# A written-out order of instructions replaced by another, with other ways of splitting numbers in its first quarter

## The chip, the cores and the metric

The kernel runs on one core of a Trainium2 chip. A core has five engines, each with its own queue of instructions that it works through in order: TensorE (PE in the profile) multiplies matrices, VectorE (DVE), ScalarE (ACT) and GpSimd (POOL) work on elements, and SyncE (SP) issues transfers. The engines wait for one another by semaphores. The metric is the time of one execution on the device in microseconds. The kernel before has a median of 1121.21 us over three runs (1118.67 to 1121.53).

## The reference

```python
def _attn_ref(q, k, v, tau):                       # (8, 8, 576, 64) each
    scale = 1.0 / np.sqrt(q.shape[-1])
    scores = scale * np.matmul(q, k.transpose(0, 1, 3, 2))
    thresh = np.max(scores, axis=-1, keepdims=True) - tau
    scores = np.where(scores >= thresh, scores, -1000000000.0)
    scores = scores - np.max(scores, axis=-1, keepdims=True)
    attn = np.exp(scores)
    attn = attn / (np.sum(attn, axis=-1, keepdims=True) + 1e-09)
    return np.matmul(attn, v).astype(np.float32)

def _moe_ref(x, w_in, w_out):                      # (4608, 512), (512, 2048), (2048, 512)
    h = x @ w_in
    pos, neg = h >= 1.0, h <= -1.0
    g = np.where(pos, h, np.where(neg, 0.0, (h + 1.0) ** 2 / 4.0))
    return (g @ w_out).astype(np.float32)
```

Attention of 8 batches with 8 heads over 576 positions, in which scores more than tau below a row's maximum are dropped, is followed by a feed-forward network (FFN) on the 4608 tokens. The weights come as 64-bit floats, the rest as 32-bit ones.

## The kernel before, in words

Most products are computed in 16-bit floats, with each operand split into a high word (the value rounded to 16 bits) and a low word (what the rounding left, again in 16 bits). Two or three products of such words replace one in 32 bits. So nearly every operand passes through a **split**: it is scaled by a power of two, its high word is written, and the low word is the difference. Most of the change is about which engine does this.

*Heads.* They are taken in pairs, four to a batch. For each pair q and k are loaded into one of seven `raw` buffers, their squares are summed on ScalarE (line 544), a small product adds the sums up (line 552), VectorE and GpSimd derive the scales, and q and k are split. `QHOW` says how, by a letter for each pair: P means scaling on GpSimd (line 572), high word on ScalarE (578), low word on GpSimd (585); D means high word on ScalarE (576) and a *fused low word* on VectorE, scaling and difference in one instruction (583). From the second batch on the words then go by DMA into `kk` and `qq`. V is split likewise (`VHOW`: P means high words on GpSimd, line 660, and a fused low word on VectorE, 667; A the high words on ScalarE, 658; N in three steps on ScalarE and GpSimd, 651, 656 and 665) and turned by a transposing DMA. V of the first batch is turned by TensorE instead (line 698).

*Tiles.* The softmax has 288 tiles of 128 rows by 576 positions, 36 to a batch. A tile's scores (line 1005) fill one of two `s` buffers in PSUM. VectorE takes the extremum (1022) and later masks and sums (1043); ScalarE does the exponential between them (1029). `TILE` gives the way of the rest by tile number, P where it says nothing. P: normalisation on GpSimd (1061), high word on ScalarE (1074), low word on GpSimd (1077). A: the normalisation goes to ScalarE (1071). D: high word on ScalarE (1083), fused low word on VectorE (1086). S: like D, with the masked values left in PSUM (1091 to 1102). T: TensorE turns the tile through a diagonal matrix that GpSimd makes (1123, 1127), and ScalarE and VectorE split the result (1130, 1133). All but T send both words through a transposing DMA (line 1105) into `eT`, which the product with V reads (1193).

*Weights.* Both matrices come in 16 tiles of 128 by 512. Line 774 loads one; three or four instructions build 32-bit floats from the bits of the 64-bit ones (`SIGN`: N puts the low bits on GpSimd, line 795, and the sign fix on ScalarE, 788; A and D put the low bits on ScalarE, 797; D needs one VectorE instruction more, 809). A product of their own (816) gives the scale (724, 727, 746). Then `CONV` says how a tile is split. G and A: scaled, rounded and subtracted in three instructions, the first two on GpSimd (860, 866) or on ScalarE (858, 864), the third on GpSimd (869). D: high word on GpSimd (875), fused low word on VectorE (878). P, Q, R, S: high word on GpSimd (875) or ScalarE (873), the difference by two products on TensorE (881, 882), and the low word copied out by ScalarE (888) or VectorE (886). M: TensorE scales (891), ScalarE and VectorE take the words (894, 897).

*FFN.* 20 groups of at most 256 tokens run in steps of four 128-column blocks: the first product (line 1265), the gate in five instructions on ScalarE and VectorE (1271 to 1288), the second product (1310), and at its end an eviction and a store. `FSCALE` says for each batch whether the factors of the gate (lines 965 to 969) are made on VectorE or on GpSimd.

*Order.* All this is recorded as some 5,440 operations. The table `ORDER` lists their numbers in the order in which they are issued; the planner walks through it, gives each operation its buffers, and emits each engine's instructions by it. So the table fixes every queue, the transfers on SP's included. In stretches where the planner expects TensorE to wait, in the first part of the program, it inserts products of ones into a free bank (line 1344), which keep the engine's clock up. Their number follows from the table.

## Time and profile before

| what | value |
| --- | --- |
| median of three runs | 1121.21 us (1118.67 to 1121.53) |
| the profiled execution: its time, its span | 1122.48 us, 1120.7 us |
| instructions | 27229 |
| busy: TensorE, VectorE, ScalarE, GpSimd | 1091.5, 898.6, 881.3, 763.4 us |
| granted clock of TensorE, mean | 0.996 |
| read from and written to main memory | 45.09 MB, 9.44 MB |

The span reaches from the first to the last instruction. A row of the profile's groups gives line, engine and operation, output and inputs with shapes, the number of instructions, their busy time in us and the mean of one in ns, and then the idle time of the engine just before them with what ended it. An engine that is off the path that sets the end may be idle at no cost.

### The profile page before, as it was taken

The numbers are of one execution on the slowest core, as the hardware profiler recorded it, in microseconds if no ns is written. First come the engines' busy times: TensorE is split into PE (matmuls) and PEld (weight loads), VectorE is DVE, ScalarE is ACT, GpSimd is POOL, SyncE is SP. The second block draws the span as 40 slices with busy tenths as digits, with TensorE's granted clock in tenths as the row PEclk, the third lists the DMA queues.
The fourth block names the chain that finished last, engine by engine and source line by source line (L and its number), as shares of the span: only waits on it lengthen the run. The fifth ranks groups of instructions, "written<-read, shape, count | busy, mean of one in ns | idle before, by whom it ended". The sixth has DMA issues, their size and how long they took to land.

```text
span 1120.7 us, 27229 instructions
## 1 busy us (share of the span) xinstructions
PE 1091.5 (97%) x9590; PEld 767.8 (69%) x9590; DVE 898.6 (80%) x2724; ACT 881.3 (79%) x1690; POOL 763.4 (68%) x879
## 2 busy tenths in 40 slices
PE   8889989999999999999999999999999999999998
PEld 7566647766777676766777677676677676767774
DVE  5999989988899788798888888888698888876322
ACT  7999989888788888878788788777788876776343
POOL 5899877566757987678767886677696986556000
PEclk9899999999999999999999999999999999999999
DMA  9997999689969999669966999559797987646000
GB/s 350 327 230 141 159 197 186 137 157 219 172 128 159 201 188 195 146 128 213 200 98 128 201 202 177 116 115 198 160 176 147 194 149 131 116 86 127 11 20 19
DMA packets 435929, 179.41 MB, mean 160 GB/s; under 512 B 400464, under 2 KB 407632, under 8 KB 435792
## 3 DMA queue, kind: packets, MB, share of 16 engines
q1 hardware_dynamic: 435792, 177.67, 77.5%
q8 instruction: 75, 1.23, 0.5%
q14 instruction: 62, 0.51, 0.1%
HBM read 45.09 MB, written 9.44 MB: 49 GB/s over the span
## 4 chain that ended last, share of the span: by engine, by line
PE 65%; DVE 10%; ACT 9%; POOL 6%; DMA 6%; issue 4%; SPq 0%; ACTq 0%; DVEq 0%; POOLq 0%
PE acc L1310 24%; PE ph L1265 24%; PE s L1005 8%; PE ph L1193 6%; DMA eT<-hl 5%; DVE s L1022 3%; DVE e L1043 2%; POOL hl L1077 2%; ACT e L1029 2%; ACT hl L1074 2%; POOL e L1061 1%; POOL nat L585 1%; PE ph L1344 1%; POOL raw L572 1%; DVE hl L1086 1%
## 5 line engine op out<-in xcount | busy, mean ns | idle before, releaser
L1077 POOL TENSOR_TENSOR hl<-e,hl 128x576 f16<-128x576 f32 x277 | 357.4, 1296 | 137.8 <-ACT hl L1074 131.5
L1265 PE MATMUL ph<-x,WI 128*128 128x256 f16 (+1 forms) x4032 | 400.9, 257 | 1.9 <-DVE gb L1288 0.8
L1265 PEld LDWEIGHTS <-WI 128*128 128x128 f16 x4032 | 347.1, 98 | 50.7 <-issue 5.3
L1022 DVE TENSOR_SCALAR_CACHE_REDUCE s<-s,pc 128x576 f32<-128x576 f32 x288 | 233.2, 818 | 42.3 <-PE s L1005 39.3
L1043 DVE SCALAR_TENSOR_TENSOR e<-s,sm,e 128x578 f32<-128x578 f32 x286 | 232.6, 815 | 41.4 <-ACT e L1029 33.3
L1029 ACT ACTIVATE e<-s,sm 128x576 f32<-128x576 f32 x288 | 211.6, 741 | 61.9 <-DVE s L1022 42.2
L1061 POOL TENSOR_SCALAR e<-e,sm 128x576 f32<-128x576 f32 x263 | 200.2, 766 | 88.0 <-DVE sm L1053 68.2
L1074 ACT ACTIVATE hl<-e 128x576 f16<-128x576 f32 x277 | 186.9, 682 | 55.0 <-POOL e L1061 30.5
L1310 PE MATMUL acc<-WO,ga 128*128 128x512 f16 x864 | 204.3, 379 | 0.0
L1005 PE MATMUL s<-kk,qq 128*128 128x288 f16 (+3 forms) x1360 | 191.9, 286 | 11.1 <-DVE e L1043 7.1
L1005 PEld LDWEIGHTS <-qq 128*128 128x128 f16 (+3 forms) x1360 | 115.5, 99 | 69.7 <-issue 22.2
L1278 DVE SCALAR_TENSOR_TENSOR ph<-ph,fcs,asq 128x512 f32<-128x512 f32 (+1 forms) x160 | 111.5, 698 | 53.7 <-ACT asq L1274 52.8
L1271 ACT ACTIVATE asq<-ph,fcs 128x512 f32<-128x512 f32 (+1 forms) x160 | 115.7, 737 | 35.6 <-PE ph L1265 34.3
L1310 PEld LDWEIGHTS <-ga 128*128 128x128 f16 x864 | 82.3, 98 | 84.4 <-issue 3.7
L1193 PE MATMUL ph<-eT,vst 128*64 128x320 f16 (+2 forms) x1928 | 123.1, 279 | 2.1 <-DVE e L1043 1.0
L1193 PEld LDWEIGHTS <-vst 128*64 128x64 f16 x1928 | 98.8, 110 | 25.0 <-issue 14.1
L1283 ACT ACTIVATE ga<-ph,fcs 128x256 f16<-128x256 f32 (+1 forms) x160 | 70.0, 448 | 29.4 <-DVE ph L1278 25.8
L1274 ACT ACTIVATE asq<-asq 128x512 f32<-128x512 f32 x144 | 90.6, 629 | 2.7
L1288 DVE SCALAR_TENSOR_TENSOR ga<-ph,fcs,ga 128x256 f16<-128x256 f32 (+1 forms) x160 | 70.6, 450 | 26.5 <-ACT WI L1283 11.7
L1310 PE MATMUL acc<-WO,gb 128*128 128x512 f16 x300 | 72.5, 379 | 0.0
L1310 PE MATMUL acc<-WO,WI 128*128 128x512 f16 x294 | 70.8, 379 | 0.0
L585 POOL TENSOR_TENSOR nat<-raw,nat 128x576 f16<-128x576 f32 x50 | 65.0, 1302 | 6.9 <-ACT nat L578 3.5
(201 smaller groups left out, 1152.9 us busy)
## 6 DMA issues: line engine op xcount, KB each, us to landing
kk<-nat SPq DMA_DIRECT2D x112, 144.0 KB, 3.0
raw<-in_v_dram SPq DMA_DIRECT2D x32, 288.0 KB, 3.8
raw<-in_q_dram SPq DMA_DIRECT2D x32, 288.0 KB, 3.8
raw<-in_k_dram SPq DMA_DIRECT2D x32, 288.0 KB, 3.4
WO<-in_moe_w_in_dram SPq DMA_DIRECT2D x16, 512.0 KB, 7.9
out_dram<-ob SPq DMA_DIRECT2D x32, 256.0 KB, 2.7
qq<-nat SPq DMA_DIRECT2D x112, 72.0 KB, 2.6
x<-in_moe_w_out_dram SPq DMA_DIRECT2D x10, 512.0 KB, 6.4
```

The costliest lines, as they stand in the source:

```text
L1005: T.matmul(ap(s, s_ps)[r, f, :SH], q, k, start=ql == kl == 0, stop=kl == 1)
L1022: V.tensor_scalar(sv(), sv(), c[:, 24 + v : 25 + v], None, ALU.mult, ALU.min, accum_out=t[:, 0:1])
L1029: A.activation(ev(), sv(), AF.Exp, bias=ap(m, sm)[:, 0:1], scale=-1.0)
L1043: V.scalar_tensor_tensor(ev(SH + 1), sv(SH + 1), t[:, 2:3], ev(SH + 1), ALU.is_le, ALU.mult, accum_out=t[:, 3:4])
L1061: G.tensor_scalar(ev(), ev(), ap(m, sm)[:, 5:6], ESC, ALU.mult, ALU.mult)
L1074: A.activation(part2(0), ev(), AF.Copy)
L1077: G.tensor_tensor(part2(w), ev(), part2(0), ALU.subtract)
L1193: T.matmul(o[hd * D : (hd + 1) * D, :n], vt[:, k, hd * D : (hd + 1) * D], t[:, kb, hd * n : (hd + 1) * n], start=m == 0, stop=m == len(blo ...
L1265: T.matmul(h[:, i], WTh["i"][:, u, wl * 512 + c * P : wl * 512 + (c + 1) * P], x[:, cc, xl, c0 : c0 + n].rearrange("p (t n) -> p t n", n=P ...
L1271: A.activation(tv()[:, :, c], hv()[:, :, c], AF.Relu, bias=fcs[:, b, 2, q : q + 1], scale=fcs[:, b, 3, q : q + 1])
L1278: V.scalar_tensor_tensor(hv()[:, :, c], hv()[:, :, c], fcs[:, b, 0, q : q + 1], tv()[:, :, c], ALU.max, ALU.min)
L1310: T.matmul(ap(ab, accs), gv(h, gl)[:, x], WTh["o"][:, fc + i, wl * 512 : (wl + 1) * 512], start=fc + i == 0 and m == 0, stop=not left[0] a ...
```

## The change

The table of the order is another one throughout, since the numbers of the operations shift as soon as one tile takes another way. Beside it the letters change. No function changes. The first run of clock-keeping products has 106 instead of 95, all together 260 instead of 199.

```diff
-CONV = {"i": "GRPGPDPPMPGRMPPP", "o": "GAPADMMARGDGGDMA"}
-SIGN = {"i": "NNADNNNAANNNAANN", "o": "ANNNAANNAANNNNNN"}
-VHOW = "PPPPAAN" + 25 * "P"
-QHOW = "DDPDPPDPPDD" + 21 * "P"
+CONV = {"i": "GAMGMGARPMGGMGRG", "o": "PGQAGPRGRDQGRADG"}
+SIGN = {"i": "DNNNANNNNDAANNAN", "o": "NNANANAAAANNNAAN"}
+VHOW = "PPPPPPPA" + 24 * "P"
+QHOW = "DDPDPPDPPPD" + 21 * "P"
...
 ORDER = [
-    0, 54, 56, 58, 60, 855, 860, 850, 865, 4, 59, 5, 57, 55, 2, 876, 61, 871, 1, 62, 63, 16, 64, 856, 857, 80, 862, 858, 861, 65, 17, 81, 863, 852,
+    54, 0, 58, 4, 60, 56, 862, 851, 5, 55, 857, 59, 867, 2, 877, 61, 872, 57, 1, 62, 887, 63, 64, 863, 882, 864, 80, 6, 852, 865, 853, 17, 75, 854,
...
-TILE = {0: "T", 1: "T", 4: "A", 10: "A", 11: "A", 12: "A", 20: "A", 21: "A", 22: "A", 24: "A", 25: "D", 27: "A", 28: "A", 29: "A", 30: "D", 34: "D", 37: "A", 38: "A", 39: "D", 43: "A", 49: "D", 52: "D", 55: "D", 59: "D", 60: "D"}
-FSCALE = "GGVVVVVV"
+TILE = {0: "T", 1: "T", 2: "A", 4: "D", 5: "A", 9: "A", 14: "A", 15: "A", 19: "A", 20: "A", 21: "A", 22: "A", 24: "D", 25: "A", 26: "A", 27: "A", 28: "A", 29: "A", 31: "D", 33: "A", 34: "A", 36: "A", 38: "A", 39: "A", 45: "A", 50: "A", 56: "A", 58: "D", 59: "A", 60: "D", 71: "S"}
+FSCALE = "GVVVVVVV"
```

Counted over the program, weight tiles split in three steps on GpSimd go from 7 to 12 (line 860), high words alone there from 13 to 7 (875), low words by TensorE from 12 to 10 (881), products that scale from 5 to 4 (891), fused low words of weights from 4 to 2 (878), of q and k from 12 to 10 (583), of tiles from 9 to 5 (1086). Tiles normalised on ScalarE go from 14 to 23 (1071), on GpSimd from 263 to 257 (1061). Shifts of single columns (lines 736 and 961) stand in both kernels in the same number.

The first place is GpSimd's queue from the first weight tiles to the diagonal of the first tile, `dge`; `WI` holds the first weights, `dgw` a diagonal of their scale. Before:

```order
L746 TENSOR_SCALAR dgw_133<-ident,wsc_i 128x128
L860 TENSOR_SCALAR WI<-WI,wsc_i 128x512
L866 TENSOR_SCALAR WI<-WI 128x512
L869 TENSOR_TENSOR WI<-WI 128x512
L860 TENSOR_SCALAR WI<-WI,wsc_i 128x512
L795 TENSOR_SCALAR WO<-WO 128x512
L520 TENSOR_SCALAR pc_117<-pc_117 128x3
L521 TENSOR_TENSOR pc_117<-pc_117 128x3
L564 TENSOR_TENSOR pc_117<-pc_117,tcs 128x2
L1123 TENSOR_SCALAR dge_135<-ident,sm_122 128x128
```

And now:

```order
L795 TENSOR_SCALAR WO<-WO 128x512 x2
L860 TENSOR_SCALAR WI<-WI,wsc_i 128x512
L746 TENSOR_SCALAR dgw_133<-ident,wsc_i 128x128
L866 TENSOR_SCALAR WI<-WI 128x512
L860 TENSOR_SCALAR WI<-WI,wsc_i 128x512
L795 TENSOR_SCALAR WO<-WO 128x512
L869 TENSOR_TENSOR WI<-WI 128x512 x2
L866 TENSOR_SCALAR WI<-WI 128x512
L564 TENSOR_TENSOR pc_117<-pc_117,tcs 128x2
L869 TENSOR_TENSOR WI<-WI 128x512
L1123 TENSOR_SCALAR dge_135<-ident,sm_122 128x128
```

Two more subtractions (line 869) and one more rounding (line 866) stand ahead of the diagonal, and the small scale columns (lines 520 and 521) come behind it.

The second place is VectorE's queue from the first turned tile (line 1133, which frees a score buffer `s`) to the extremum of the third tile (line 1022). Before:

```order
L1133 TENSOR_TENSOR eT_98<-s_62,eT_98 128x5x128
L803 SCALAR_TENSOR_TENSOR WI<-ph_64,WO 128x512
L1133 TENSOR_TENSOR eT_98<-s_61,eT_98 128x5x128
L457 TENSOR_SCALAR ph_63<-ph_63 128x6
L458 TENSOR_SCALAR ph_63<-ph_63 128x6
L459 TENSOR_SCALAR pc_119<-ph_63 128x6
L559 TENSOR_SCALAR pc_119<-ph_63 128x6
L878 SCALAR_TENSOR_TENSOR WI<-WI,wsc_i 128x512
L803 SCALAR_TENSOR_TENSOR WI<-ph_64,WO 128x512
L803 SCALAR_TENSOR_TENSOR WI<-ph_65,WO 128x512
L1022 TENSOR_SCALAR s_61,sm_124<-s_61,pc_117 128x2x288
```

And now:

```order
L1133 TENSOR_TENSOR eT_98<-s_61,eT_98 128x5x128
L809 SCALAR_TENSOR_TENSOR WI<-WO,ph_65 128x512
L805 SCALAR_TENSOR_TENSOR WI<-WO,ph_63 128x512
L805 SCALAR_TENSOR_TENSOR WI<-WO,ph_64 128x512
L961 TENSOR_SCALAR scs<-scs 128x1 x2
L1133 TENSOR_TENSOR eT_98<-s_62,eT_98 128x5x128
L803 SCALAR_TENSOR_TENSOR WI<-ph_63,WO 128x512
L583 SCALAR_TENSOR_TENSOR qq_84<-raw_70,pc_118,qq_84 128x576
L803 SCALAR_TENSOR_TENSOR WI<-ph_65,WO 128x512
L1022 TENSOR_SCALAR s_61,sm_124<-s_61,pc_117 128x2x288
```

Three instructions on the bits of weights and two columns now stand between the two turned tiles, where one stood, and a low word of q (line 583) follows in place of one of weights (line 878).

The third place is VectorE's queue where the two orders meet; `ga` and `gb` are buffers of the gate's output. Before:

```order
L1288 SCALAR_TENSOR_TENSOR ga_110<-ph_63,fcs,ga_110 128x256
L1288 SCALAR_TENSOR_TENSOR gb_113<-ph_63,fcs,gb_113 128x256
L1278 SCALAR_TENSOR_TENSOR ph_64<-ph_64,fcs,asq_100 128x512
L583 SCALAR_TENSOR_TENSOR nat_76<-raw_75,pc_118,nat_76 128x576
L1026 TENSOR_SCALAR sm_124<-sm_124,tcs 128x1
L1288 SCALAR_TENSOR_TENSOR ga_108<-ph_64,fcs,ga_108 128x256
L1288 SCALAR_TENSOR_TENSOR gb_114<-ph_64,fcs,gb_114 128x256
L1043 SCALAR_TENSOR_TENSOR e_94,sm_124<-s_61,sm_124,e_94 128x578
```

And now:

```order
L1288 SCALAR_TENSOR_TENSOR WO<-ph_65,fcs,WO 128x256
L1278 SCALAR_TENSOR_TENSOR ph_64<-ph_64,fcs,asq_101 128x512
L1053 RECIPROCAL sm_126<-sm_126 128x1
L1022 TENSOR_SCALAR s_61,sm_122<-s_61,pc_121 128x2x288
L1026 TENSOR_SCALAR sm_122<-sm_122,tcs 128x1
L1288 SCALAR_TENSOR_TENSOR ga_109<-ph_64,fcs,ga_109 128x256
L1288 SCALAR_TENSOR_TENSOR gb_113<-ph_64,fcs,gb_113 128x256
L1043 SCALAR_TENSOR_TENSOR e_94,sm_122<-s_61,sm_122,e_94 128x578
```

From line 1026 on, the fifth row before and now, the rows are the same in both to the end, but for the numbers of the buffers. The other engines have such a place too; on SP it lies 438 rows from the end.

## The prediction

> **What bounds the kernel now.** I read the page first, for its busy shares and for the chain that ended last.

> ```profile
> PE 1091.5 (97%) x9590; PEld 767.8 (69%) x9590; DVE 898.6 (80%) x2724; ACT 881.3 (79%) x1690; POOL 763.4 (68%) x879
> ...
> PE 65%; DVE 10%; ACT 9%; POOL 6%; DMA 6%; issue 4%; SPq 0%; ACTq 0%; DVEq 0%; POOLq 0%
> ```

> TensorE is busy for 1091.5 of 1120.7 us, and two thirds of the chain is its own work. What can still be won is therefore TensorE's idle time and work taken off it. Where the idle time lies is shown by the busy time of each engine in stretches (columns: stretch, its length, then each engine's busy us with its instructions, granted clock, DMA share, GB/s).

> ```profile
> 0.00:28.00 28.00, 22.92 (x255) 19.68 (x256) 15.85 (x49) 20.51 (x44) 15.28 (x55) 0.99 0.94 350
> 28.00:56.00 28.00, 23.43 (x167) 14.20 (x167) 25.75 (x89) 26.06 (x51) 24.09 (x35) 0.89 0.90 327
> 56.00:84.00 28.00, 24.91 (x319) 17.29 (x317) 27.16 (x97) 26.52 (x51) 26.50 (x36) 1.00 1.01 230
> 84.00:112.00 28.00, 25.53 (x355) 19.22 (x353) 26.35 (x91) 27.62 (x56) 26.37 (x30) 1.00 0.80 142
> 112.00:140.00 28.00, 26.71 (x309) 19.16 (x307) 26.70 (x77) 25.58 (x46) 23.10 (x28) 1.00 0.92 159
> 140.00:168.00 28.00, 25.00 (x172) 13.48 (x171) 23.89 (x79) 24.97 (x49) 19.89 (x23) 1.00 0.95 197
> 168.00:196.00 28.00, 27.15 (x232) 21.03 (x230) 26.50 (x77) 25.21 (x46) 20.17 (x23) 1.00 1.01 186
> 196.00:224.00 28.00, 27.80 (x264) 20.82 (x263) 26.92 (x83) 23.44 (x45) 14.85 (x15) 1.00 0.68 137
> 448.00:560.00 112.00, 112.00 (x916) 78.22 (x915) 94.13 (x286) 90.19 (x170) 85.93 (x94) 1.00 0.87 171
> 1092.00:1121.00 29.00, 23.93 (x171) 13.04 (x168) 8.35 (x24) 10.79 (x27) 0.00 (x0) 0.97 0.07 19
> ```

> Up to 196 us TensorE is idle for 5.1 + 4.6 + 3.1 + 2.5 + 1.3 + 3.0 + 0.9 = 20.4 us. From 196 us on it is all but full (27.80 of 28, later 112.00 of 112), until the last 29 us, where 5.1 us go to the last gates and the last store. So there are two regimes. In the first 196 us the other engines set the pace: from 28 to 112 us VectorE is busy for 79.3 of 84 us, ScalarE for 80.2 and GpSimd for 77.0. Afterwards TensorE does. The waits say the same of the first regime (columns: who waited for whom, us in total, times, longest).

> ```profile
> PE s L1005 <- DVE e L1043: 7.1, 13, 1.2
> ...
> PE s L1127 <- POOL dge L1123: 1.3, 1, 1.3
> ```

> The score matmuls wait for VectorE to free one of the two score buffers; that is the largest wait of TensorE, and it is small and scattered. How far the softmax tiles have come is counted by their first VectorE instruction, which the profile shows as two records to a tile:

> ```profile
> 0.00:112.00 112.00, 21.44 (x50) 0.97 0.91 262
> 112.00:196.00 84.00, 21.45 (x50) 1.00 0.96 181
> 196.00:224.00 28.00, 8.72 (x20) 1.00 0.68 137
> ```

> So some 25 tiles have passed at 112 us, 50 at 196 us and 60 at 224 us. I use this to turn places in the order into times.

> **The change part by part.** The first finding comes from the order alone: on every engine the rows after a certain place are the same in both kernels but for the turn of the buffers. On VectorE these are the last 1480 or so rows, on ScalarE the last 1120, on GpSimd the last 608; on TensorE everything from the score matmuls that stand at about 277 us of the profile. The place on VectorE lies at tile 75 (the low word of line 583 just ahead of it), and that on TensorE behind an attention product:

> ```profile
> 272.08 0.81 DVE L583 SCALAR_TENSOR_TENSOR nat<-raw,pc,nat 128x576 f16<-128x576 f32 x1
> ...
> 275.56 2.09 PE L1193 MATMUL ph<-eT,vst 128*64 128x320 f16 x28
> ```

> There TensorE is already full. So the 840 us behind it, the end included, cost what they cost now, and the change is worth exactly what TensorE gains or loses before 277 us. I take the terms in that part.

> *TensorE's own work.* Two weight tiles fewer have their low word made by TensorE (line 881 and 882), and one fewer is scaled there (line 891); the clock-keeping matmuls of line 1344 grow from 199 to 260.

> ```profile
> L1344 PE MATMUL ph<-ones 128*128 128x128 bf16 x179 | 13.5, 243 | 2.4 <-POOL ones L468 2.3
> L881 PE MATMUL ph<-WI,dgw 128*128 128x512 f32 x20 | 12.1, 687 | 1.6 <-ACT WI L888 1.3 <-DVE WO L805 0.3
> L882 PE MATMUL ph<-WI,minus 128*128 128x512 f16 x10 | 4.0, 404 | 0.0
> L891 PE MATMUL ph<-WI,dgw 128*128 128x512 f32 x4 | 2.2, 632 | 0.1
> ```

> An fp32 matmul is two records, so one pass of line 881 costs 12.1 / 10 = 1.21 us, one of line 882 0.40, one of line 891 2.2 / 2 = 1.1. Removed: 2 x (1.21 + 0.40) + 1.1 = 4.3 us. Added: 61 x 13.5 / 179 = 4.6 us of clock-keeping, all of it before 84 us, where TensorE has 12.7 us of idle time to put it in. Up to the scores of tile 56 these are the only lines of TensorE whose counts differ; from there to the common part the two queues hold the same matmuls. What are 4.3 us less work worth? At most -4.3 us, if TensorE set the pace before tile 56, and 0 if it waits for others all the way. The nearest row is the wait for VectorE (7.1 us), and the splits fall where TensorE idles 20.4 us. I take 0 and keep -4.3 for the range.

> *The start.* The first run of clock-keeping matmuls grows from 95 to 106, and the matmul that sums V's squares (line 633) stands behind it in the queue.

> ```profile
> 2.32 7.57 PE L1344 MATMUL ph<-ones 128*128 128x128 bf16 x95 [2.32 <-POOL ones L468]
> 8.63 0.18 ACT L627 ACTIVATION_READ_ACCUMULATOR junk<-raw 128x1 f32 x1
> 9.73 0.17 PE L633 MATMUL ph<-vssq,ones 128*128 128x4 bf16 x1
> ```

> The last square was read out at 8.81 us, and line 633 began only at 9.73, when the 95 were through: the filling already sets this start. Eleven more at 7.57 / 95 = 0.08 us make it 0.9 us later, and VectorE and GpSimd both begin on its result. Term: +0.9 us. It would be 0 if the queues behind it had slack to give back.

> *VectorE before tile 56.* I counted its rows up to the first instruction of tile 56 in both orders, each at its mean.

> ```profile
> L667 DVE SCALAR_TENSOR_TENSOR vb<-raw,scs,vb 128x576 f16<-128x576 f32 x27 | 31.6, 1171 | 0.9 <-POOL vb L660 0.5 <-issue 0.3
> L1086 DVE SCALAR_TENSOR_TENSOR hl<-e,sm,hl 128x576 f16<-128x576 f32 x9 | 8.8, 986 | 0.5 <-POOL pc L520 0.4
> L878 DVE SCALAR_TENSOR_TENSOR WO<-WO,wsc_o 128x512 f16<-128x512 f32 x3 | 3.3, 1106 | 0.0
> L897 DVE TENSOR_TENSOR WO<-ph,WO 128x512 f16<-128x512 f32 x3 | 2.1, 684 | 0.0
> ```

> The after order has there two fused low words of tiles fewer (-2.0) and two of weights fewer (-2.1), but one of V more (+1.2), two low words from TensorE's output more and one less (+0.7; line 886 is not in this trace, and I give it line 897's 0.68), one more gate of the FFN (+0.7), one more softmax mask (+0.9), one more scale of line 965 to 969 on VectorE (+0.9 by then) and one weight tile more whose sign takes two steps (+0.7); the rest are one-column instructions (+1.9 together). The net is +2.9 us at tile 56; it is +3.7 at tile 20, +2.6 at tile 44, and -2.1 where the orders meet, since its lighter tiles come late. A mean also counts overlap with the next instruction: two records of a tile's minimum have 818 + 141 ns by their means and 21.44 / 25 = 858 ns by the stretch above, 0.89 of it. So VectorE, which is 94% busy and on which the score buffers wait, reaches tile 56 about 2.9 x 0.89 = 2.6 us later. Bounds: 0, if its idle time of 6.9 us between 112 and 196 us (84 - 26.70 - 23.89 - 26.50) takes it all, and +3.3 for tile 20. I let 1.0 us be taken up there: +1.6 us.

> *ScalarE* has 3.2 us more by tile 56, mostly six or seven more normalisations (line 1071):

> ```profile
> L1071 ACT ACTIVATE e<-e,sm 128x576 f32<-128x576 f32 x14 | 11.0, 786 | 0.0
> ```

> That lies beside VectorE's extra and is of its size; I add nothing for it. Without that cover it would be the 3.2 us itself.

> *GpSimd.* Five more weight tiles are split here in three steps and six fewer in one.

> ```profile
> L869 POOL TENSOR_TENSOR WI<-WI 128x512 f16<-128x512 f32 x3 | 3.5, 1159 | 0.2
> L860 POOL TENSOR_SCALAR WI<-WI,wsc_i 128x512 f32<-128x512 f32 x3 | 2.1, 694 | 0.0
> L866 POOL TENSOR_SCALAR WO<-WO 128x512 f16<-128x512 f32 x4 | 2.8, 712 | 0.3
> L875 POOL TENSOR_SCALAR WI<-WI,wsc_i 128x512 f16<-128x512 f32 x9 | 6.2, 695 | 0.3
> L1061 POOL TENSOR_SCALAR e<-e,sm 128x576 f32<-128x576 f32 x263 | 200.2, 766 | 88.0 <-DVE sm L1053 68.2 <-DVE sm L1026 7.8 <-ACT asq L1271 3.4
> ```

> Up to tile 36 that is 5 x (1.16 + 0.70 + 0.71) - 6 x 0.70 = +8.7 us, with three duplications of V more (+3.7), five normalisations fewer (-3.8) and three conversions of raw bits fewer (-2.0): about +7 us, and by the full count +7.8. By tile 16, near 80 us, it is +4.5. GpSimd is idle for 5.4 us from 28 to 84 us and for 20.1 us from 28 to 168 us, so the extra just fits, and I cost it at 0. It hides under VectorE's own 94%; if its idle time cannot be used, it costs what the second rival says. One place is exposed: the diagonal of the first tile (line 1123) now stands behind two more subtractions of line 869, 2.3 us, and TensorE waited 1.3 us for it already. VectorE's rows before the first two tiles are freed grow as well, by 4 us, so both arrive late together.

> *The clock.* In two slices the clock was down while TensorE was in demand:

> ```profile
> 28.00:32.00 4.00, 4.00 (x24) 2.98 (x23) 2.96 (x9) 3.16 (x7) 3.50 (x5) 0.67 0.99 364
> 36.00:40.00 4.00, 3.69 (x18) 1.94 (x18) 3.90 (x12) 3.96 (x8) 3.55 (x8) 0.68 1.04 412
> ```

> TensorE lost 4 x (0.33 + 0.32) = 2.6 us there, and VectorE stood idle for 1.04 us in the first slice. The after order has fewer splits on TensorE and more filling at this place. I take back VectorE's 1.0 us; the bounds are 0 and -2.6.

> *Contention.* A fused low word of line 1086 took 0.80 to 1.81 us:

> ```profile
> L1086 DVE SCALAR_TENSOR_TENSOR hl<-e,sm,hl x9: 801/818/1806, 111.7 to 231.8; 128x576 f16<-128x576 f32 x9
> ```

> The mean of 0.986 stands 0.17 above the median; eight fewer of lines 1086, 878 and 583 save some 1.4 us of stretching, which their means above include. [...]

> The single-column shifts of the change's name are in both kernels alike (the same counts on lines 736 and 961) and cost nothing. Weight scales on GpSimd (line 965) go from two to one.

> **The sum**: 0 + 0.9 + 1.6 + 0 - 1.0 = +1.5 us. The profiled execution took 1122.48 us (span 1120.7), 1.3 us above the median of the three runs, 1121.21. Against its own time the changed kernel would take 1124.0; against the median 1122.7. A measurement of this kernel can tell about 0.3%, 3.4 us, from no change, so the forecast is no change.

> **The rivals.** *TensorE sets the pace from 84 us on.* For it: 25.53, 26.71, 25.00 and 27.15 of 28 us, and the waits for VectorE are short. Then the 4.3 us of removed work come off, the late VectorE rows hide, and with the clock's 2.6 and the start's 0.9 it is -4.3 to -6.0: 1115 to 1117 us, faster. Against it: VectorE and ScalarE are as full in these stretches, and the removed splits lie mostly before 84 us, where TensorE idles.

> *GpSimd becomes the bound from 40 to 140 us.* Its subtractions (line 1077) feed the transposes, and its splits feed the first FFN steps. It decides once GpSimd's idle time of 5.4 us between 28 and 84 us cannot fall below 0.9 us: +4.5 us by then, +7.8 at tile 36. Part of the 7.8 is given back between 140 and 224 us, where it idles for 8.1, 7.8 and 13.2 us. With the start's 0.9 the time is 1126 to 1130 us, slower. For it: 26.50 and 26.37 of 28 us already, in order and full of waits for ScalarE. Against it: the normalisations moved off it, and its place in the waits of TensorE is one wait of 1.3 us.

> *The new order has a bad place of its own*, a late load or a transpose queued behind another in the common ring of buffers. In order of time the chain of now holds this transpose among others:

> ```profile
> 152.26 5.00 DMA eT<-hl
> ```

> One such exposed is +5 us, one removed is -5.

> *The change does nothing because nothing of it lies on the path* gives 1121 and cannot be told from the forecast.

> **How the numbers follow.** Forecast, with the case of nothing: 0.43. TensorE sets the pace: 0.22. GpSimd becomes the bound: 0.22. A bad or a mended place: 0.13, in halves a little to the slow side. That gives 0.27 for faster by over 0.3%, 0.43 for within, 0.30 for slower. The forecast's own range is 1119 to 1125; since the other cases hold over half, the range reaches from TensorE's 1115.5 to 1130, the upper end of GpSimd's.

> **What would show it.** Right: the same idle of TensorE behind 280 us; line 633 at 10.6 us; tile 56 later by 1 to 3 us; TensorE's idle up to 196 us near 20.4 plus the 4.3 us of work removed. TensorE's pace: that idle stays at 20 us, and the common part begins earlier than 277 us. GpSimd's: over 27.5 of 28 us busy from 56 to 112 us, and waits of ScalarE or TensorE for lines 1061, 1077 or 1123 that grow by microseconds. Wrong altogether: differences that arise behind 300 us, where the orders agree.

## The result and the profile after

The changed kernel took 1130.30 us (median of four runs, 1128.08 to 1132.49), the kernel before, run beside it, 1121.37 us (1118.67 to 1121.84). The ratio is 1.0071, with an interval of 1.0045 to 1.0096. The change made the kernel slower by about 0.7%, 8 to 9 us. The forecast was 1122.7 and no change; the result lies 0.3 us above the upper end of its range.

The profiled execution took 1129.07 us, with a span of 1127.3 us, 6.6 more than before. The page's first row:

```profile
PE 1097.0 (97%) x9643; PEld 774.1 (69%) x9643; DVE 895.9 (79%) x2731; ACT 884.3 (78%) x1695; POOL 772.7 (69%) x883
```

TensorE is busy for longer than before (1091.5 us), although 4.3 us of its work, by the rows before, were taken off. The products of ones took 20.9 us where they took 14.9, so 6.0 us more and not the 4.6 that their number gave. This is the largest of their rows:

```profile
L1344 PE MATMUL ph<-ones 128*128 128x128 bf16 x239 | 19.4, 248 | 3.0 <-POOL ones L468 2.3 <-DVE WI L803 0.7
```

The stretches (columns as in the prediction) show where:

```profile
0.00:28.00 28.00, 23.53 (x241) 19.13 (x242) 15.57 (x48) 20.03 (x44) 16.13 (x55) 0.90 0.96 352
28.00:56.00 28.00, 21.44 (x224) 14.92 (x223) 25.83 (x95) 26.66 (x50) 25.51 (x39) 0.97 0.82 295
56.00:84.00 28.00, 24.66 (x206) 15.03 (x206) 24.50 (x81) 24.16 (x45) 22.18 (x30) 0.64 0.93 232
84.00:112.00 28.00, 27.47 (x416) 22.78 (x415) 24.71 (x91) 25.35 (x51) 25.57 (x30) 0.94 0.79 139
112.00:140.00 28.00, 26.89 (x264) 17.30 (x262) 26.72 (x85) 26.89 (x49) 24.82 (x27) 1.00 0.82 151
140.00:168.00 28.00, 25.09 (x225) 16.11 (x223) 23.97 (x75) 24.28 (x48) 20.13 (x24) 1.00 1.03 182
168.00:196.00 28.00, 27.34 (x230) 20.24 (x229) 24.80 (x74) 24.81 (x44) 19.84 (x20) 1.00 1.10 196
```

TensorE's idle time up to 196 us is 19.6 us, where it was 20.4, so it does not wait for longer. But its granted clock is 0.90 from 0 to 28 us, where it was 0.99, and 0.64 from 56 to 84 us, where it was 1.00. In the latter stretch VectorE, ScalarE and GpSimd are busy for 24.50, 24.16 and 22.18 of 28 us, where they were for 27.16, 26.52 and 26.50. In a finer cut, two stretches of the changed kernel and then the same of the kernel before:

```profile
57.00:75.00 18.00, 16.73 (x103) 9.33 (x100) 14.66 (x48) 14.53 (x26) 13.23 (x16) 0.53 0.95 235
81.00:88.00 7.00, 7.00 (x63) 5.97 (x61) 6.64 (x21) 5.38 (x10) 6.50 (x13) 0.53 0.94 244
```

```profile
57.00:75.00 18.00, 14.91 (x176) 9.33 (x173) 17.56 (x64) 17.76 (x34) 17.32 (x22) 1.00 0.96 232
81.00:88.00 7.00, 5.79 (x97) 4.71 (x95) 6.01 (x20) 6.07 (x12) 6.41 (x12) 1.00 1.05 182
```

In these two spells TensorE ran at half clock, for 17 us and for 7 us. It was busy almost without a break there, and the others waited for it. A spell that is as long as the second lies earlier, from 22.7 to 29.5 us, and makes the 0.90 of the first stretch:

```profile
23.00:29.00 6.00, 6.00 (x35) 3.95 (x35) 5.54 (x18) 5.35 (x13) 5.74 (x8) 0.50 1.04 405
```

In the kernel before, the only spells until the very end were two of 3.4 us, from 27.2 and from 37.5 us on. The waits from 57 to 75 us in the changed kernel (who waited for whom, us, times, longest):

```profile
DVE s L1022 <- PE s L1005: 2.4, 2, 1.7
...
ACT WI L888 <- PE ph L882: 1.6, 1, 1.6
...
ACT ph L797 <- PE ph L1344: 0.9, 1, 0.9
```

VectorE waited for scores, ScalarE for a low word made on TensorE, and ScalarE also for a bank in which products of ones (line 1344) were still running. In the kernel before, no wait for TensorE is listed there. Just ahead of the two later spells, and in them, TensorE's rows in order of time (start, us, the instructions, and in brackets the idle time before them) are these:

```profile
54.65 0.91 PE L1005 MATMUL s<-kk,qq 64*128 64x288 f16 x6 [0.72 <-DVE e L1043]
55.92 0.89 PE L1005 MATMUL s<-kk,qq 64*128 64x288 f16 x6 [0.36 <-DVE e L1043]
...
60.20 1.60 PE L1005 MATMUL s<-kk,qq 64*128 64x288 f16 x6 [1.27 <-DVE e L1043]
...
78.82 1.03 PE L1193 MATMUL ph<-eT,vst 128*64 128x128 f16 x30 [2.06 <-DVE WO L805]
...
83.27 4.87 PE L1265 MATMUL ph<-x,WI 128*128 128x128 f16 x48
```

Single microseconds of the same trace date the spells (columns as above):

```profile
56.00:57.00 1.00, 1.00 (x9) 0.65 (x9) 1.00 (x2) 0.92 (x3) 0.74 (x2) 0.91 0.88 344
57.00:58.00 1.00, 1.00 (x13) 1.00 (x11) 1.00 (x4) 0.71 (x1) 1.00 (x1) 0.50 1.01 414
73.00:74.00 1.00, 1.00 (x6) 0.40 (x4) 0.00 (x0) 1.00 (x3) 0.25 (x1) 0.56 1.04 283
74.00:75.00 1.00, 1.00 (x11) 0.70 (x10) 0.90 (x5) 1.00 (x3) 0.00 (x0) 1.00 1.07 196
80.00:81.00 1.00, 1.00 (x10) 0.68 (x9) 1.00 (x2) 1.00 (x5) 1.00 (x2) 0.85 0.65 70
```

TensorE waited 0.72 and 0.36 us, and the clock fell at about 56.8 us; it came back near 73.9. TensorE waited 2.06 us, and the clock fell at 80.7. The first FFN step (line 1265) took 4.87 us, where it took 2.84 before.

The product behind which the two queues are alike began 5.1 us later than before (275.56 us), and the rest of the span is 1.5 us longer. TensorE's row of it:

```profile
280.65 2.09 PE L1193 MATMUL ph<-eT,vst 128*64 128x320 f16 x28
```

In this pair of executions the start got hardly later. Line 633 began at 9.80 us, where it began at 9.73, since the 106 products of ones took 7.64 us, where the 95 took 7.57 (rows in order of time):

```profile
2.33 7.64 PE L1344 MATMUL ph<-ones 128*128 128x128 bf16 x106 [2.33 <-POOL ones L468]
9.80 0.17 PE L633 MATMUL ph<-vssq,ones 128*128 128x4 bf16 x1
```

So the question for the experiments was whether the half clock was the cause or only went along with another one: GpSimd's extra splits, or the order itself.

### The profile page after: what moved, and what is told of

Its sections match the earlier page's. It is cut to its first block, busy times and chain, and to the rows that moved or that the text cites. A ratio compares the mean times of both kernels' runs of the same rounds, so it can differ in the third digit from the quotient of the medians.

```text
span 1127.3 us, 27377 instructions
## 1 busy us (share of the span) xinstructions
PE 1097.0 (97%) x9643; PEld 774.1 (69%) x9643; DVE 895.9 (79%) x2731; ACT 884.3 (78%) x1695; POOL 772.7 (69%) x883
## 4 chain that ended last, share of the span: by engine, by line
PE 71%; DVE 7%; DMA 7%; POOL 6%; ACT 5%; issue 3%; SPq 0%; ACTq 0%; POOLq 0%; DVEq 0%
PE ph L1265 26%; PE acc L1310 26%; PE s L1005 10%; PE ph L1193 7%; DMA eT<-hl 4%; POOL hl L1077 2%; DVE s L1022 2%; DVE e L1043 2%; POOL e L1061 1%; DMA raw<-in_q_dram 1%; ACT hl L1074 1%; PE ph L1344 1%; DMA WO<-in_moe_w_in_dram 1%; ACT e L1029 1%; ACT asq L1271 1%
## 5 line engine op out<-in xcount | busy, mean ns | idle before, releaser
L1043 DVE SCALAR_TENSOR_TENSOR e<-s,sm,e 128x578 f32<-128x578 f32 x285 | 231.8, 815 | 37.9 <-ACT e L1029 29.3
L1061 POOL TENSOR_SCALAR e<-e,sm 128x576 f32<-128x576 f32 x257 | 195.8, 767 | 91.8 <-DVE sm L1053 73.0
L1005 PE MATMUL s<-kk,qq 128*128 128x288 f16 (+3 forms) x1360 | 193.0, 290 | 11.3 <-DVE e L1043 9.6
L1005 PEld LDWEIGHTS <-qq 128*128 128x128 f16 (+3 forms) x1360 | 116.0, 100 | 73.1 <-issue 26.5
L1271 ACT ACTIVATE asq<-ph,fcs 128x512 f32<-128x512 f32 (+1 forms) x160 | 115.9, 737 | 39.0 <-PE ph L1265 37.1
L1310 PEld LDWEIGHTS <-ga 128*128 128x128 f16 x864 | 82.2, 98 | 83.7 <-issue 3.0
L1193 PE MATMUL ph<-eT,vst 128*64 128x320 f16 (+2 forms) x1928 | 123.1, 281 | 4.0 <-DVE WO L805 2.1
L1193 PEld LDWEIGHTS <-vst 128*64 128x64 f16 x1928 | 99.6, 111 | 26.9 <-issue 17.5
L585 POOL TENSOR_TENSOR nat<-raw,nat 128x576 f16<-128x576 f32 x52 | 67.4, 1297 | 10.4 <-ACT nat L578 10.0
```

The costliest lines, as they stand in the source:

```text
L1005: T.matmul(ap(s, s_ps)[r, f, :SH], q, k, start=ql == kl == 0, stop=kl == 1)
L1043: V.scalar_tensor_tensor(ev(SH + 1), sv(SH + 1), t[:, 2:3], ev(SH + 1), ALU.is_le, ALU.mult, accum_out=t[:, 3:4])
L1061: G.tensor_scalar(ev(), ev(), ap(m, sm)[:, 5:6], ESC, ALU.mult, ALU.mult)
L1193: T.matmul(o[hd * D : (hd + 1) * D, :n], vt[:, k, hd * D : (hd + 1) * D], t[:, kb, hd * n : (hd + 1) * n], start=m == 0, stop=m == len(blo ...
L1271: A.activation(tv()[:, :, c], hv()[:, :, c], AF.Relu, bias=fcs[:, b, 2, q : q + 1], scale=fcs[:, b, 3, q : q + 1])
L1310: T.matmul(ap(ab, accs), gv(h, gl)[:, x], WTh["o"][:, fc + i, wl * 512 : (wl + 1) * 512], start=fc + i == 0 and m == 0, stop=not left[0] a ...
```

## The experiments

Each run's kernel was timed against the kernel before on the same chip. Times are medians, ratios go to the kernel before.

**More products of ones in the planned gaps.** The first theory was that the clock fell because the fillings were too few or too short.

```diff
+            mid = 30 < o.t < 100
...
-            if o.t - free > WARM[0] and o.t < WARM[1]:
+            if o.t - free > (0.15 if mid else WARM[0]) and o.t < WARM[1]:
...
-                    found += [(free, bank, min(gap, end - free)) for ...
+                    found += [(free, bank, max(min(gap, end - free), 14*WARM[3] if mid else 0.0)) for ...
```

In a_keep14, above, the runs planned between 30 and 100 us have at least 14 products; a_mid1 fills the same gaps for their whole planned length instead (`gap = (1.0 if mid else WARM[2]) * (o.t - free)`).

> The changed kernel with more clock-keeping products between the planned times 30 and 100 us (344 instead of 260: twelve runs of 14 each in place of 9, 12, 14, 9, 6, 6, 11, 6, 6, 5); nothing else differs. Clock theory (the half clock of TensorE at 57 to 75 and 81 to 88 us, 0.53 in both stretches, holds the tiles up and is worth the 5.1 us by which the common part begins late): the clock stays above 0.9 from 56 to 84 us and the time falls by 4 to 9 us, to 1121 to 1126 us. Row theory (the rows that VectorE and GpSimd have more before tile 36 make it late, and the slow clock is only what a waiting TensorE shows): the clock may rise, and the time stays within 2 us of the changed kernel's 1130, since the same rows are in the same queues.

> The changed kernel with the filling of planned gaps from 30 to 100 us raised from three quarters to all of them, and gaps from 0.15 us filled (292 products instead of 260). Clock theory: a weaker dose of the same; if it holds the clock up from 56 to 84 us, the time is that of the strong dose within 2 us; if the clock still falls, the time stays near 1130, and the two doses differ as the clock does. Row theory: no difference between the doses and from the changed kernel beyond 2 us.

a_keep14 took 1129.55 us (ratio 1.0055, 1.0033 to 1.0076), a_mid1 1130.32 (1.0080, 1.0057 to 1.0102). A stretch of a_keep14, and then the two largest waits in TensorE's rows in order of time:

```profile
56.00:84.00 28.00, 23.41 (x213) 14.60 (x212) 23.49 (x78) 23.59 (x44) 21.53 (x26) 0.72 0.84 220
```

```profile
61.24 1.48 PE L1005 MATMUL s<-kk,qq 64*128 64x288 f16 x6 [2.20 <-DVE e L1043]
...
81.11 1.14 PE L1193 MATMUL ph<-eT,vst 128*64 128x128 f16 x30 [2.39 <-DVE WO L805]
```

The clock from 56 to 84 us was 0.72 and 0.65 (0.64 in the changed kernel). More filling in the gaps that the planner expects did not hold it. The second fence fits this: the waits ahead of the spells, now 2.20 and 2.39 us, were left unfilled. Since the clock did not rise, these two runs do not tell the clock theory from the row theory.

**Less filling in the kernel before.**

```diff
-WARM = (0.4, 200, 0.75, 0.056)
+WARM = (0.4, 30, 0.75, 0.056)
```

> The kernel before without the clock-keeping products planned behind 30 us (166 instead of 199: the runs of 13, 8 and 12 are gone); its order is as it was. Clock theory: if the clock falls between 40 and 84 us, which it did not before (1.00 from 56 to 84), the time rises by 3 to 8 us although no row of the order moved; if it does not fall, the time stays. Row theory: the time stays within 2 us of 1121 either way.

It took 1121.74 us (1.0015, 0.9993 to 1.0038). In the profiled execution the clock was 1.00 from 56 to 140 us, so the order of before can hold it there without any product of ones behind 30 us. It does not always: over the ten executions the mean clock went from 0.998 down to 0.989, and the time from 1120.0 up to 1131.1 us.

**The splits alone.** In the kernel before, five tiles of the first weights go from letter P (low word by TensorE) to G (three steps on GpSimd):

```diff
-CONV = {"i": "GRPGPDPPMPGRMPPP", ...
+CONV = {"i": "GRGGPDGPMGGRMGPG", ...
```

> The kernel before with five weight tiles of the first matrix split in three steps on GpSimd instead of through TensorE (the letters of tiles 2, 6, 9, 13 and 15 are G instead of P), in the order of before; the clock-keeping products follow from the table and grow to 290. This is the change's splitting on GpSimd alone: 5 x (1.16 + 0.70 + 0.71 - 0.70) = 9.4 us more on GpSimd before tile 16, TensorE 5 x 1.6 = 8.0 us less. Row theory: GpSimd, 92% busy there, becomes the bound and the time rises by 4 to 9 us. Clock theory: the time rises only if the clock falls between 40 and 90 us; with the clock at 1.00 it rises by under 3 us.

It took 1132.67 us (1.0096, 1.0073 to 1.0119): this part alone, in the old order, costs about as much as the whole change (the intervals overlap). Two stretches of this run, then waits from 28 to 112 us:

```profile
28.00:56.00 28.00, 19.53 (x180) 13.28 (x179) 24.37 (x82) 20.50 (x40) 25.46 (x36) 0.82 0.86 319
56.00:84.00 28.00, 23.65 (x272) 16.66 (x270) 23.28 (x81) 24.29 (x47) 27.01 (x34) 0.88 0.81 192
```

```profile
PE acc L816 <- DVE WI L805: 3.3, 1, 3.3
...
ACT WI L873 <- POOL WI L869: 4.0, 1, 4.0
...
PE s L1127 <- POOL dge L1123: 2.4, 1, 2.4
```

The clock fell to 0.82 and 0.88, and GpSimd was busy for 27.01 of 28 us. So either could be the cause, and the next two runs take the two halves of this edit apart.

**GpSimd's half, and TensorE's half.**

b_pool writes five high words (line 875) four times over; b_noPE leaves out the scaled product of the same five tiles:

```diff
+                    for _ in range(4 if w == "i" and u in (2, 6, 9, 13, 15) else 1):
                         G.tensor_scalar(hi, src, s, 1.0, ALU.mult, ALU.mult)
...
+                if w == "i" and u in (2, 6, 9, 13, 15):
+                    T.matmul(ap(lb, ph), minus, hi, start=True, stop=True)
+                    return
```

> The kernel before, in which GpSimd writes the high word of five weight tiles (2, 6, 9, 13 and 15 of the first matrix, line 875) four times over: 15 instructions of about 0.70 us more on GpSimd, 10.5 us in all, all in the first 100 us, where the run that moved the splits of these tiles from TensorE to GpSimd added 9.4 us. TensorE keeps all its work. If GpSimd's load is what costs: about what that run cost, 1129 to 1133 us, and the clock in the stretches from 28 to 112 us falls as there, since TensorE waits more. If the work taken off TensorE is what costs, by the clock: 1121 to 1124 us and a clock of 0.98 to 1.00 from 56 to 112 us.

> The kernel before, in which the difference of the same five weight tiles leaves out the scaled product (line 881, 1.21 us each, 6.0 us in all); the product of line 882 and the copy stay, so the low words of these tiles are not the reference's. No other engine has more or less to do. If the work taken off TensorE lets its clock fall, and that costs: a clock of 0.8 to 0.95 somewhere in 28 to 112 us, and 1125 to 1131 us. If GpSimd's load was what cost: the clock as before, and 1115 to 1121 us, since TensorE has 6 us less to do.

b_pool took 1132.33 us (1.0098, 1.0080 to 1.0117), b_noPE 1124.43 (1.0021, 1.0008 to 1.0035). Two stretches of b_pool and waits from 28 to 112 us, and then the same of b_noPE:

```profile
28.00:56.00 28.00, 20.77 (x107) 12.85 (x106) 22.03 (x74) 20.96 (x41) 22.70 (x35) 0.74 0.78 285
56.00:84.00 28.00, 22.38 (x192) 12.57 (x192) 21.34 (x74) 21.08 (x40) 26.49 (x34) 0.85 0.60 161
```

```profile
PE s L1128 <- POOL dge L1124: 3.4, 2, 2.1
...
PE ph L883 <- POOL WI L876: 3.2, 2, 2.2
```

```profile
28.00:56.00 28.00, 21.85 (x161) 13.89 (x161) 25.13 (x87) 25.82 (x51) 25.47 (x36) 0.77 0.91 329
56.00:84.00 28.00, 23.87 (x261) 15.88 (x260) 24.68 (x88) 25.00 (x47) 23.33 (x28) 0.82 0.92 202
```

```profile
PE ph L882 <- POOL WI L875: 2.2, 1, 2.2
```

Both expectations hit in part and missed in part. GpSimd's extra work in the old order costs 10.6 us, though TensorE keeps its work, because it stands ahead of the diagonal (line 1124 in this run, 1123 before) and of the product with the high word (883, before 882), for both of which TensorE waits; the clock falls too, to 0.74. And with 6.0 us less on TensorE and nothing more anywhere, the kernel got 2.7 us slower, not faster: the product that was left out had covered a wait for GpSimd's high word, which now shows as 2.2 us (line 882 is the product that is left there), and the clock fell to 0.77 and 0.82. So a split on TensorE can also be a cover for a wait.

**Wider products of ones** in the changed kernel, behind the first run of 106.

```diff
+            T.matmul(bank, ones, ones[:, :1].to_broadcast([P, k * P]), start=True, stop=True)
```

> The changed kernel, with its clock-keeping products behind the first run taken 512 columns wide (one column of ones repeated) in place of 128, a quarter as many, in the same places and the same free banks. Less of the time of such a product goes into loading weights. If what the clock follows is how many columns stream, rather than how many products are issued: the clock from 56 to 84 us rises from 0.64 to over 0.85, and if the clock is what costs, the time falls to 1121 to 1126 us. If the waits of TensorE decide the clock: it stays at 0.6 to 0.75 there, and the time at 1128 to 1132 us.

1130.61 us (1.0073, 1.0052 to 1.0094). The stretch in question:

```profile
56.00:84.00 28.00, 24.42 (x181) 12.53 (x181) 24.33 (x83) 23.80 (x44) 21.71 (x29) 0.64 0.90 232
```

The clock from 56 to 84 us is 0.64 again, with 12.53 us of weight loads where the changed kernel had 15.03. Wider products in the same places do not hold it either.

**GpSimd relieved in the changed kernel.**

```diff
-                else:
+                elif w == "o":
                     G.tensor_scalar(src, src, s, 1.0, ALU.mult, ALU.mult)
...
+                if how == "G" and w == "i":
+                    G.tensor_scalar(hi, src, s, 1.0, ALU.mult, ALU.mult)
+                elif how == "A":
...
+                if w == "i" and CONV[w][u] == "G":
+                    G.tensor_scalar(lo, src, s, 1.0, ALU.mult, ALU.mult)
+                    return
                 G.tensor_tensor(lo, src, hi, ALU.subtract)
```

> The changed kernel with GpSimd's work on the seven tiles of the first weights that it splits in three steps cut to two: the scaling (line 860) is left out, the high word is made as on line 875, and in place of the subtraction (1.16 us) stands a second copy of the high word (0.70 us), so the low words of these tiles are not the reference's. GpSimd has 7 x 1.17 = 8.2 us less to do, about the 7.8 us that the change gave it; the other engines' rows stay. If GpSimd's load is the cause, through waits that then halve the clock: 1119 to 1124 us, the clock from 56 to 84 us over 0.85. If the cause is the TensorE work that was taken off, or waits for VectorE: the clock still falls there, and 1126 to 1131 us.

1131.03 us (1.0070, 1.0049 to 1.0090): nothing was won. Two stretches of it:

```profile
28.00:56.00 28.00, 23.11 (x188) 14.35 (x188) 25.47 (x91) 24.93 (x48) 18.96 (x32) 0.81 0.84 297
56.00:84.00 28.00, 23.24 (x236) 14.23 (x232) 23.61 (x81) 24.15 (x45) 21.77 (x28) 0.74 0.75 194
```

GpSimd is far from full in both stretches (in the changed kernel the first had 25.51 us), and the clock falls all the same, to 0.81 and 0.74 (0.97 and 0.64 in the changed kernel). So in the order of the change the extra time of the splits on GpSimd is not what was lost, and what such work cost in the old order does not carry over. That the new order puts the splits where less waits for them may be the reason; no run shows it.

**Products of ones where TensorE waits.** In the changed kernel they are put ahead of the very rows whose waits preceded the spells, into columns of a bank that nobody reads, so that they wait for nothing. A key of the table below is an operation's number, the value the count of products ahead of it (a_spot, then a_spot2):

```diff
+        spot = {1235: 9, 1225: 5, 1248: 28, 1245: 30}
         for o in order:
+            for _ in range(spot.get(o.n, 0)):
+                T.matmul(accs[0][:, 256:384], ones, ones, start=False, stop=False)
...
+        spot = {1235: 9, 1225: 5, 1248: 32, 1258: 12, 1281: 10, 1245: 56}
```

> The changed kernel with 72 more products of ones at four places of TensorE's queue, where it waited in the profile: 9 and 5 ahead of the two score passes that began at 54.65 and 55.92 us, 28 ahead of the one at 60.20, 30 ahead of the attention product at 78.82. They go into columns of the accumulator's bank that nobody reads, and wait for nothing. All engines' other rows stay. They fill 0.07 us each, 5.0 us in all, of waits of 4.4 us in the changed kernel's own trace. If the clock is what costs, and TensorE's waits of 1.3 to 2.2 us let it fall: the granted clock from 56 to 84 us rises from 0.64 to over 0.85, lines 1022 and 1271 no longer wait for TensorE there, and the time is 1121 to 1126 us. If GpSimd's later rows cost by themselves: whatever the clock does, 1128 to 1131 us.

> The changed kernel with the products of ones at four places of TensorE's waits, now 9, 5, 32 and 56 of them, and 12 and 10 more ahead of the score passes that began at 62.65 and 68.29 us in the run with four places. There one spell of half clock was left, from 76.6 to 83.5 us, behind a window with 1.6 us of waits; its time was 1125.9 us against 1130.3 of the changed kernel. If the clock explains what the four places gave back: no spell between 40 and 140 us, 1122 to 1125 us. If they helped in another way: 1125.5 to 1127, whether this spell goes or not. What then remains above 1121.7 is not the clock's.

a_spot took 1125.94 us (1.0031, 1.0015 to 1.0047), a_spot2 1127.86 (1.0060, 1.0046 to 1.0075). Stretches of a_spot, then of a_spot2:

```profile
28.00:56.00 28.00, 21.86 (x234) 15.04 (x234) 26.58 (x96) 26.83 (x51) 26.02 (x39) 1.00 0.85 310
56.00:84.00 28.00, 23.48 (x285) 17.54 (x283) 26.46 (x89) 25.62 (x46) 25.16 (x34) 0.88 1.06 230
...
140.00:168.00 28.00, 26.26 (x193) 16.14 (x192) 23.89 (x77) 24.34 (x47) 19.41 (x25) 0.94 1.00 178
```

```profile
28.00:56.00 28.00, 22.73 (x235) 15.36 (x233) 26.27 (x95) 26.61 (x51) 25.93 (x40) 0.94 0.81 292
56.00:84.00 28.00, 24.91 (x356) 19.53 (x356) 25.76 (x87) 25.36 (x47) 24.78 (x33) 1.00 1.03 248
...
140.00:168.00 28.00, 25.55 (x173) 15.54 (x174) 21.77 (x70) 22.20 (x44) 17.83 (x22) 0.88 0.85 160
```

The long spell is gone in both, and in a_spot2 the one from 76.9 to 83.7 us too. In a_spot nothing was changed but that TensorE got 72 products more to do, and the kernel gained 4.4 us. So the waits do bear on the clock here, and a filling that stood in them held it better: 0.88 from 56 to 84 us, where it was 0.64. In a_spot the first FFN step began 3.2 us earlier than in the changed kernel, though it still fell into that spell, as its row in order of time shows:

```profile
80.12 4.54 PE L1265 MATMUL ph<-x,WI 128*128 128x128 f16 x48
```

But a_spot2 missed what was expected of it. With a clock of 1.00 from 56 to 84 us it should have gained on a_spot, and lost 1.9 us. Its profiled execution had spells at 23.9 and 37.6 us that a_spot's had not, and one of 6.8 us from 146.8 us on, behind the wait in the row below. The first two lie ahead of all the added products, as does the changed kernel's own at 22.7 us, which a_spot's trace lacks too. So part of the difference between two traces is one between executions, not between kernels.

```profile
146.20 2.66 PE L1005 MATMUL s<-kk,qq 64*128 64x288 f16 x12 [2.40 <-DVE e L1043]
```

So one trace per kernel is not enough to go by.

**Less filling in the changed kernel** (the edit of b_fill30).

> The changed kernel with clock-keeping products only up to 30 us of the planned time. Behind that, 23 of them stood in the spell of half clock from 57 to 74 us, where they took 3.0 us of TensorE's time and ScalarE waited 1.4 us for the banks that they write. If TensorE is the bound in that spell: 2 to 3 us less, 1126 to 1128.5 us, at the same clock. If the products still keep part of the clock: a longer spell of half clock and 1130 to 1136 us. If neither (GpSimd sets the pace): 1130, the same.

1127.46 us (1.0049, 1.0035 to 1.0062), 2.8 us less than the changed kernel. The stretch from 56 us:

```profile
56.00:84.00 28.00, 22.45 (x186) 12.94 (x184) 25.78 (x88) 25.85 (x48) 23.80 (x31) 0.66 0.89 238
```

This is what was expected if TensorE is the bound in the spells: the clock is 0.66, about the same, TensorE is busy for 22.45 us where it was for 24.66, and the other three do more than in the changed kernel. Products of ones that don't hold the clock cost time there. Over the executions the mean clock was no higher than the changed kernel's (0.9845 and 0.9855), so these 2.8 us are not the clock's. The intervals of the two ratios overlap; but the means of a_mid1, a_wide and a_lessG, at 1130.1 to 1130.4 us, lie with the changed kernel's 1130.3, and this run's is 1127.5.

**The same spots in the kernel before**, as a version that might beat both (74 products at six waits between 25 and 49 us):

```diff
+        spot = {1163: 8, 1160: 18, 1186: 7, 1176: 6, 1209: 18, 973: 17}
```

> The kernel before with 74 products of ones (0.07 us each) at six places where TensorE waited for 0.4 to 1.3 us in its own profile: ahead of the score passes at 25.38, 34.98, 36.31 and 44.20 us, of the turned tile at 27.57 and of the split at 48.63. It had two spells of half clock, at 27.6 to 31.4 and 37.7 to 41.1 us. If waits set the clock and the clock is on the path there: no spell from 25 to 50 us and 1118.5 to 1121 us. If the spells in this stretch lie beside waits for other engines: the clock rises and the time stays within 1120.5 to 1123. If products of ones this early stand in the way: 1123 to 1125.

1122.31 us (1.0008, 0.9999 to 1.0018). The two spells of the kernel before, at 27.2 and 37.5 us, are gone (1.00 from 0 to 84 us), and the time did not move; others came at 111.4 and 152.4 us. This is what was expected if spells lie beside waits for other engines: a higher clock is not always worth time. No version tried beats the kernel before.

**Execution by execution.** Every timed execution comes with its mean granted clock, and the same kernel does not always get the same one. This holds the program and the order fixed. It is no experiment, though: what lowers the clock, a longer wait for instance, may also cost time by itself. The nine executions of a_keep14, by clock:

```
clock 0.985 0.986 0.986 0.986 0.990 0.991 0.993 0.993 0.994
us    1130.60 1130.37 1130.01 1130.59 1129.55 1128.77 1124.04 1125.99 1125.09
```

Five us lie between a clock of 0.986 and one of 0.993. Over all 177 executions of the fourteen kernels, each measured from the mean of its own kernel, 0.001 less of mean clock goes with 0.59 us more (95% interval 0.46 to 0.71). In three of the fourteen (b_noPE, a_lessG, b_spot), whose clocks differ by 0.006 at most, the slope is flat or the other way, and the clock accounts for about a third of the scatter within the kernels. With 0.59, the means can be brought to one clock, 0.996, that of the kernel before in the profile:

| kernel | executions | mean us | mean clock | at 0.996 |
| --- | --- | --- | --- | --- |
| before | 75 | 1122.1 | 0.9950 | 1121.5 |
| after | 4 | 1130.3 | 0.9855 | 1124.1 |
| a_keep14, a_mid1, a_wide | 19 | 1128.3, 1130.4, 1130.1 | 0.9893, 0.9862, 0.9840 | 1124.4, 1124.6, 1123.1 |
| a_lessG | 6 | 1130.4 | 0.9848 | 1123.8 |
| a_spot, a_spot2 | 18 | 1125.9, 1128.1 | 0.9934, 0.9937 | 1124.4, 1126.7 |
| a_fill30 | 12 | 1127.5 | 0.9845 | 1120.8 |
| b_fill30, b_spot | 21 | 1123.6, 1122.5 | 0.9950, 0.9972 | 1123.0, 1123.2 |
| b_G5, b_pool | 10 | 1132.2, 1132.8 | 0.9887, 0.9878 | 1127.9, 1128.0 |
| b_noPE | 12 | 1124.2 | 0.9893 | 1120.3 |

Between before and after the clock differs by 0.0095, which is 5.6 us (4.4 to 6.7) of the 8.2 us between the means. Some 2.6 us remain at equal clock. They are uncertain by about 3 us, since kernels that differ from the changed one by products of ones alone spread from 1120.8 to 1126.7, so they are not told from nothing. The two edits that gave the clock back price it without the slope: a_spot got 4.4 us for 0.0079 and a_spot2 2.2 us for 0.0082, which makes 5.2 and 2.5 us for 0.0095. b_G5 and b_pool keep 6.4 and 6.5 us at equal clock, so there, by this reckoning, GpSimd's work itself was the greater part; relieving GpSimd in the changed kernel (a_lessG) gives 0.3 us. The last column is an extrapolation, the longest one for a_fill30, which without its products of ones has the lowest clock.

## Why the prediction was wrong, step by step

*What bounds it, and the common part: right.* The loss arose before the place where the orders meet: 5.1 of 6.6 us in the profiled executions. The other 1.5 us lie within what executions differ by: from the extremum of the 81st tile to the end the fourteen traces took 822.0 to 826.6 us, the kernel before 823.2 and the changed one 824.9. That TensorE waits for VectorE in the first 196 us was right as well, but not complete: at half clock the others waited for TensorE (2.4, 1.6 and 0.9 us from 57 to 75 us in the changed kernel).

*The clock: the step that failed.* The prediction read two slices at 0.67 and 0.68 in the trace of before, put the price of a spell at 1.0 to 2.6 us, and took 1.0 back, since "the after order has fewer splits on TensorE and more filling at this place". Neither reason holds. Work taken off TensorE uncovered a wait (b_noPE, in the old order: 6.0 us of work off, 2.7 us slower), and the filling in planned gaps, which is meant to keep the clock up, did not (a_keep14, a_mid1, a_wide: 0.72, 0.65 and 0.64 from 56 to 84 us). The clock fell further, and the term was about +5.6 us by the slope, +2.5 to +5.2 by the two edits, in place of -1.0. With the first of these the sum of +1.5 becomes +8.1, against 8.2 between the means. That the two agree so well is luck, as the next points show. What makes TensorE wait ahead of the spells stays open: by the rows these waits ended on VectorE (lines 707, 1043 and 805), and no run put the splits back on TensorE or took rows off VectorE in the new order.

*TensorE's own work, 0.* For the removed work the value may be near: brought to equal clock by the slope, b_noPE's 6.0 us were worth 1.2 us, so 4.3 would be worth about 0.9, but b_noPE's own executions do not show that slope. What it missed is that such work can cover waits, as in b_noPE (2.2 us). For the added products of ones it was too low: they were to fit into idle time for nothing, and leaving out those behind 30 us gave back 2.8 us at no higher clock (a_fill30).

*The start, +0.9.* The profiled pair hides it: 9.80 against 9.73 us, with 0.072 us for a product of ones in place of 0.080. The clock first rose at 5.61 us in the one and at 6.75 in the other. Up to there the products began 0.106 us apart in both, behind it 0.056, so more of them ran at full clock: 74 of 106 and 53 of 95. That moment differs from execution to execution. Over all traces line 633 began at 9.51 us on the mean with 95 products in the first run (six traces) and at 10.21 with 106 (eight), 0.7 us later, so the size was about right. What it is worth at the end no run shows.

*VectorE, +1.6.* The 57th record of the extremum (line 1022) came at 212.7 us before and at 218.6 after; in a_spot, with most of the clock back, at 216.4. The 2.6 us that remain at equal clock are what the rows gave before I let 1.0 be taken up (2.9 x 0.89). This fits, but no run took the VectorE rows away, so it is not shown; what remains may as well be the 2.8 us of the products of ones, or waits of the new order. The 2.40 us for a mask (line 1043) in a_spot2's row at 146.20 us is one.

*GpSimd, 0.* Right for this order as far as one run shows: a_lessG gave nothing back, and GpSimd was busy for 22.18 and 25.57 of 28 us from 56 to 112 us, not for the 27.5 that its rival named. That rival's time, 1126 to 1130, nearly came out, but by another cause. In the old order its price was real (b_pool, 10.6 us), so idle time of 5.4 us in a stretch did not mean that 4.5 us more fit: added instructions stood in front of rows for which TensorE then waited 3.4 and 3.2 us.

*Contention and the single columns.* No run told them apart from the rest, and none shows what made one row of line 1086 take 1.81 us. The fused low words did not get longer with more work on GpSimd: up to the common part lines 583, 667, 878 and 1086 took 974 ns on the mean before (28 instructions) and 913 after (21).

*The chances.* Slower had 0.30. The mechanism that came, TensorE losing its clock so that the others wait for it, was not among the rivals; the prediction had the half-clock slices in its own quoted rows and treated them as something that filling cures.

## What to carry to other kernels

Before taking work off TensorE, look at what that work covers: in b_noPE a wait of 2.2 us showed once 6.0 us of work were gone, the clock fell to 0.77 and 0.82 in two stretches of 28 us, and the kernel got 2.7 us slower. If products are inserted to hold a clock, put them where the trace shows the waits (a_spot: 0.88 from 56 to 84 us in place of 0.64, and 4.4 us less), not where a planner expects gaps (a_keep14, a_mid1, a_wide: 0.72, 0.65, 0.64), and leave out those that do not hold it (a_fill30: 2.8 us less). And when the same kernel gets different clocks from run to run, plot time against clock within one kernel: it gives a first estimate of the clock's share without a single edit. An edit has to confirm it, since one cause can move both.

## What the runs showed of the hardware

```profile
32.92:36.33 3.41, 1.86 (x17) 1.42 (x14) 3.27 (x11) 3.05 (x6) 2.48 (x6) 1.00 1.03 412
53.40:56.81 3.41, 2.33 (x23) 1.38 (x21) 3.24 (x14) 3.41 (x8) 3.17 (x5) 1.00 0.94 208
```

Behind the first the clock stayed, behind the second it fell. So these traces show no sharp limit in idle time alone, but it counts. Over the first 300 us of all fourteen traces, cut into windows of one step on the grid of the clock's changes:

| TensorE's idle time in a window at full clock | windows | followed by half clock |
| --- | --- | --- |
| under 1.0 us | 705 | 1 |
| 1.0 to 1.4 us | 54 | 17 |
| 1.4 to 2.0 us | 24 | 17 |
| over 2.0 us | 13 | 13 |

Being busy by the records did not by itself bring the clock back: in the long spell TensorE was busy almost throughout (16.73 of 18 us) and stayed at half clock for 17 us, and of the 70 half-clock windows without idle time 29 were followed by another. And a lost clock cost about half of what it took here, by the slope: 0.001 of the mean clock is 1.1 us of full-clock time over the run, and it cost 0.59 us.
